# Moving twelve output products from iteration 10 of a slot into its second group, and a transfer of A's factors behind the rows of maxima

## The chip, the core and the metric

The kernel runs on one core of a Trainium2 chip. The metric is the time on the device in microseconds (us), as the median of several executions. The profile comes from one further execution, whose own time stands beside its span below. Engines are named as in the profile: PE (TensorE, matmuls), PEld (its weight loads), DVE (VectorE), ACT (ScalarE), POOL (GpSimd), and SP (SyncE), which here issues the DMAs of the main loop. A number such as L590 is a line of the kernel.

## The reference

Two attentions over the same input x (2048 rows of 512, 32 heads of 16) are mixed by a gate. A is a causal softmax attention within four chunks of 512 rows, mixed per head with a linear memory of the chunks before. B is a plain softmax attention over all 2048 rows. Each is multiplied with its output weights.

```python
def _A_ref(x, wq, wk, wv, wo, beta):
...
    for s in range(N):
        qs, ks, vs = q[:, :, s], k[:, :, s], v[:, :, s]
        logits = jnp.einsum("bhqd,bhkd->bhqk", qs, ks) * scale + mask
        p = _softmax(logits, axis=-1)
        a_dot = jnp.einsum("bhqk,bhkd->bhqd", p, vs)
        pq = phi(qs)
        num = jnp.einsum("bhld,bhde->bhle", pq, M)
        den = jnp.einsum("bhld,bhd->bhl", pq, z)[..., None] + 1e-6
        a_mem = num / den
        o = g * a_mem + (1.0 - g) * a_dot
...
    return o @ wo

def _B_ref(x, wqkv, wo):
...
    scores = jnp.einsum("bhqd,bhkd->bhqk", q, k) * (Dh ** -0.5)
    p = _softmax(scores, axis=-1)
    o = jnp.einsum("bhqk,bhkd->bhqd", p, v)
    return (lambda x, *d: x.transpose(*d))(o, 0, 2, 1, 3).reshape(B, S, D) @ wo

x = A_x
g = _sigmoid((x * gate_w).sum(-1, keepdims=True))
a = _A_ref(x, A_wq, A_wk, A_wv, A_wo, A_beta)
b = _B_ref(x, B_wqkv, B_wo)
return g * a + (1 - g) * b
```

## The kernel before

A first stage computes the projections and the memory of A and stores queries, keys and values to DRAM. Then comes the main loop (L905): 32 **slots**, k = 0 to 31. Slot k works on one unit of B (unit 32 + k) and one of A (unit k); a unit is four heads against one chunk of 512 query rows. The order of all instructions is written out by hand: the loop records them one after another, each engine executes its own in that order, and semaphores make it wait for the others. SP, too, executes its DMA issues strictly in that order.

A slot has 37 **groups** n: 32 of B (two for each of 16 blocks of 128 keys; n // 2 is the iteration "it") and five of A. For each group the loop records, in this order:

- `t_group` (L490): two score products on PE into two PSUM banks, and two exponentials on ACT (L508) that read these banks and write the probabilities. Three banks, tb, tb and mb, take turns by which was used longest ago; `misc()` hands out the same three for other work. In A's groups POOL masks the result (L511).
- what `plan` holds for the group: as a rule one `s_b` (L441), two products on PE into a double bank sbk, and a maximum over them on DVE (L450). These maxima belong to the *next* slot's unit of B; there are two double banks.
- what `extras` (L848) holds for it as "pre": in slots 9 to 31 one `out_mm` at group 2 x OMI = 20, and in slot 31 a second one at group 28.
- `pvs` (L826): the products of the probabilities with V (L524), two groups behind the scores. Group 0 has the last ones of A's unit of the slot before and then the copy of A's sums out of PSUM (L531). Group 1 has none.
- what `extras` holds as "post": `m_rows` at group 24.
- after the odd groups, `beside` (L860) and some loads.

`out_mm` (L586) is half an output projection for 128 rows: twelve products of 512 columns (L590) of oh and ol, the two halves in precision of the normalised sums, with the weights. For a = 0 (odd slots) ACT copies the result to yo (L594), for a = 1 (even slots) DVE adds the second half (L597) and SP stores yo (L598). oh and ol are made by `out_split` (L582) at the end of an even slot, by ACT and POOL.

`m_chain` (L454, recorded after group 21) turns the maxima into rows with four small DVE operations (L459 to L469), `m_rows` (L471, group 24) transposes them on PE, copies them on ACT and stores them by four DMAs (L483) into the operands of the following units.

The sums of a unit are normalised in steps: `fin_load` loads sums and denominators, `fin_rec` makes the factors and stores them to DRAM (L554), `fin_bc` (L556) loads them again, repeated over 16 partitions, into the tile d (L560), and `fin_norm` (L562) multiplies on POOL (L564; for A, from the second chunk on, it also adds B's part, L569). `beside` sets the iteration of each of these: B's `fin_bc` in iteration 6, A's in 7; `fin_norm` in even slots for B in 9 and for A in 13.

Of the kernel before, what the change touches and what calls it, by code (L numbers as in the profile page):

```python
# [26 lines left out]
EARLY = 6  # L27
S_FIRST = 10
S_LAST = 10
OMI = 10  # L30


@with_exitstack
def gated_mix_kernel(ctx, tc, x, wq, wk, wv, wo, beta, wqkv, wob, gate_w, out):
# [510 lines left out]
    def fin_rec(u):  # L545
        kd, qd, c = UN[u]
        r = AT.pop(("r", u))
        nc.vector.reciprocal(r, r)
        if kd == "A":
            nc.vector.scalar_tensor_tensor(r, r, nq[:, qd:qd + 1], grow[:, 0, c], op0=OP.mult, op1=OP.mult)  # L550
        else:
            nc.vector.tensor_tensor(r, r, grow[:, 1, c], op=OP.mult)
        AT["rd", u] = D.tile([128, E], FT, name=f"rd{u}")
        nc.sync.dma_start(AT["rd", u], r)  # L554
# [7 lines left out]
    def fin_norm(kd, g, c):  # L562
        o, d = AT["o"][c % 2][:, g, int(kd == "B")], AT["d"][int(kd == "B")]
        nc.gpsimd.tensor_tensor(o, o, d, op=OP.mult)  # L564
        if kd == "B":
            if c:
                nc.sync.dma_start(d, OM[g, c])
        elif c:
            nc.gpsimd.tensor_tensor(o, o, AT["d"][1], op=OP.add)  # L569
# [12 lines left out]
    def out_split(c, t):  # L582
        nc.scalar.activation(AT["oh"], o_cols(c, t), AF.Copy)
        nc.gpsimd.tensor_tensor(AT["ol"], o_cols(c, t), AT["oh"], op=OP.subtract)
# [19 lines left out]
    def tail_split(t, gs, a, eng=None):  # L604
        oh, ol = [x[:, gs, a] for x in tail_ops(t)]
        o = o_cols(3, t)[:, gs, a]
        if eng:
            nc.scalar.copy(oh, o)
        else:
            nc.vector.tensor_copy(oh, o)  # L610
        (eng or nc.vector).tensor_tensor(ol, o, oh, op=OP.subtract)
# [20 lines left out]
    def todo(fn, *a):  # L632
        return lambda: fn(*a)
# [86 lines left out]
    for blk in range(16):  # L720
# [12 lines left out]
        n = blk + 1 + (c == 2)  # L733
# [114 lines left out]
    def extras(k):  # L848

        pre, post = {}, {}  # L850
        if not k:
            for n in range(4):
                pre[2 * n] = [fill[n - 4]]
        post[2 * S_LAST + 4] = [todo(m_rows, k + 1)]
        for n, it in [(k - 9, OMI)] + [(23, 14)] * (k == 31):
            if n >= 0:
                pre[2 * it] = [todo(out_mm, n // 8, n // 2 % 4, n % 2)]
        return pre, post

    def beside(k, it):  # L860

        for f, it0, u in ((fin_load, NT + 1, 32 + k), (fin_rec, 5, 31 + k), (fin_bc, 6, 31 + k),
                          (fin_load, 1, k - 1), (fin_rec, 6, k - 1), (fin_bc, 7, k - 1)):
            if it == it0 and (k or it0 > NT):
                f(u)
        c, j = divmod(k - 1, 8)
        if k and j % 2:
            for kd, it0 in (("B", 9), ("A", 13)):
                if it == it0:
                    fin_norm(kd, j // 2, c)  # L870
        if k >= 8 and k % 2 == 0 and it == NT + 2:
            out_split(k // 8 - 1, k // 2 % 4)
        if (k, it) == (31, 4):
            grest = AT["grest"] = AT["o"][0][64:, 0, 0]
            nc.sync.dma_start(grest, GD[3 * C:].rearrange("(o t) -> o t", o=1).to_broadcast([64, C]))
        if (k, it) == (31, 9):
            grest = AT["grest"]
            nc.vector.tensor_scalar(grest, grest, nh[64:, 3:4], None, op0=OP.mult)
        if (k, it) == (31, NT + 2):
            fin_rec(63)  # L880
        if k == 31 and it == 13:
            o = AT["o"][1][:64, 3, 0]
            nc.gpsimd.tensor_tensor(o, o, AT["d"][0][:64], op=OP.mult)
        if k == 31 and it < 8 and it % 2 == 0:
            for a in range(2):
                tail_split(it // 2, slice(0, 3), a)


    ex = [extras(k) for k in range(32)]
    plan = {}  # L890

# [13 lines left out]
    for k in range(32):  # L905
        ua, ub = k, 32 + k
        banks = T3 + [SBK[0][:, n] for n in range(2)] * (k == 31)
        for n in range(NG):
            it = n // 2 if n < NG - 1 else NT + 2
# [6 lines left out]
            if n % 2 == 0 and n < NG - 1:  # L916
                continue
            beside(k, it)
            if it == S_LAST:
                m_chain(k + 1)  # L920
# [74 lines left out]
```

## Time and profile before

| | |
|---|---|
| time, median of 3 runs | 2007.81 us (2006.12 to 2014.9) |
| time of the profiled execution | 2007.75 us |
| its span, first to last instruction | 2006.0 us |
| granted TensorE clock | 0.995 |
| output products (L590), on banks tb and mb | 60 + 60 + 60 and 36 + 36 + 36 in the profile |
| one addition to yo on DVE (L597) | 692 ns, 12 times |
| one copy to yo on ACT (L594) | 597 ns, 12 times |
| one split on POOL (L584) | 2370 ns, 12 times |

How to read it: "busy" counts an engine's own instructions without its issues and waits. In a timeline a row is: start in us, duration in us, engine, line, operation, out<-in, shapes, count; in brackets stands the idle time of that engine just before, and what ended it. Rows of equal instructions that follow each other are merged, so a row with x2 covers the first one's start to the second one's end. Matmuls are pipelined, so the durations of PE's rows overlap.

### The profile page before, as it was taken

What the parts mean: (1) busy time and instruction counts of PE and PEld (TensorE: products, weight loads), DVE (VectorE), ACT (ScalarE), POOL (GpSimd) and SP (SyncE); (2) the same over time, 40 slices, a digit from 0 to 9 for tenths busy, and PEclk for the clock granted to TensorE, in tenths of its full rate; (3) what the DMA queues carried; (4) which work ended last, traced back from release to release, by engine and by line L of the source; (5) the groups of instructions that cost most, each with busy time, mean ns of one, the idle gap of its engine ahead of it and who ended that gap; (6) DMA issues with size and microseconds to landing.
All of it is one profiled execution on the core that took longest, in us unless ns stands there. A gap on an engine that the chain in (4) does not pass through costs nothing.

```text
span 2006.0 us, 43688 instructions
## 1 busy us (share of the span) xinstructions
PE 1956.3 (98%) x17517; PEld 949.0 (47%) x17517; DVE 1631.9 (81%) x1825; ACT 1435.1 (72%) x2703; POOL 256.6 (13%) x474
## 2 busy tenths in 40 slices
PE   8999999999999999999999999999999999999988
PEld 7777777444444344444444444444444444444434
DVE  6135665799999999999999999999899999899832
ACT  3233332688888888888787888787878787878883
POOL 2200000011110101111111111111111111111111
PEclk9999999999999999999999999999999999999999
DMA  7765656644443445343435344444444545444101
GB/s 222 164 190 177 197 180 177 148 106 112 95 112 85 104 93 109 81 110 81 109 79 112 85 112 85 112 85 112 85 112 85 112 85 111 85 112 85 50 26 54
DMA packets 162743, 222.49 MB, mean 111 GB/s; under 512 B 39261, under 2 KB 89453, under 8 KB 156781
## 3 DMA queue, kind: packets, MB, share of 16 engines
q1 hardware_dynamic: 159596, 211.70, 43.9%
q0 software_dynamic: 2944, 8.00, 2.2%
q8 instruction: 138, 2.26, 0.5%
q14 instruction: 65, 0.52, 0.1%
HBM read 148.21 MB, written 68.16 MB: 108 GB/s over the span
## 4 chain that ended last, share of the span: by engine, by line
PE 89%; DMA 3%; DVE 3%; ACT 2%; SPq 2%; issue 1%; POOL 0%; ACTq 0%; POOLq 0%; DVEq 0%
PE pvb L524 31%; PE tb L502 17%; PE sbk L448 12%; PE mb L502 8%; PE tb L279 3%; PE sbk L427 2%; PE tb L590 2%; PE mb L279 2%; ACT raw L508 2%; PE pvb L279 2%; DVE mxb L450 2%; PE sbk L430 2%; PE mb L590 1%; PE sbk L279 1%; PE tb L262 1%
## 5 line engine op out<-in xcount | busy, mean ns | idle before, releaser
L450 DVE TENSOR_REDUCE mxb<-sbk 128x2 f32<-128x1024 f32 x1024 | 1222.7, 1222 | 49.4 <-PE sbk L448 45.7
L508 ACT ACTIVATE raw<-tb 128x512 f32<-128x512 f32 x1557 | 886.0, 596 | 172.8 <-PE tb L502 85.6
L524 PE MATMUL pvb<-raw,vb 128*17 128x256 f32 (+1 forms) x8072 | 639.5, 389 | 0.0
L508 ACT ACTIVATE raw<-mb 128x512 f32<-128x512 f32 x780 | 465.2, 596 | 81.6 <-PE tb L502 57.5
L502 PE MATMUL tb<-qb,xh 64*128 64x512 f32 x880 | 330.9, 494 | 3.7 <-ACT raw L508 3.7
L524 PEld LDWEIGHTS pvb<-raw,vb 128*17 128x17 f32 x8072 | 133.8, 95 | 344.8 <-issue 338.4
L448 PE MATMUL sbk<-xh,qb 64*128 64x512 f32 x1344 | 287.6, 400 | 4.4 <-DVE mxb L450 3.3
L511 POOL TENSOR_SCALAR_AFFINE_SELECT raw<-raw 128x256 f32<-128x256 f32 (+1 forms) x320 | 115.4, 361 | 879.9 <-ACT raw L508 871.9
L502 PE MATMUL mb<-qb,xh 64*128 64x512 f32 x437 | 215.6, 493 | 2.0 <-ACT raw L508 2.0
L502 PEld LDWEIGHTS tb<-qb,xh 64*128 64x128 f32 x880 | 124.7, 183 | 190.5 <-issue 98.3
L502 PE MATMUL tb<-qb,kb 64*128 64x512 f32 x463 | 176.0, 496 | 4.8 <-ACT raw L508 2.8
L434 DVE TENSOR_REDUCE mx<-sbk 128x2 f32<-128x768 f32 (+1 forms) x128 | 139.8, 1092 | 43.9 <-PE sbk L430 36.2
L448 PE MATMUL sbk<-kb,qb 64*128 64x512 f32 x704 | 152.9, 408 | 0.8 <-DVE mxb L450 0.7
L448 PEld LDWEIGHTS sbk<-xh,qb 64*128 64x128 f32 x1344 | 138.8, 186 | 10.8 <-DVE mxb L450 7.0
L502 PEld LDWEIGHTS mb<-qb,xh 64*128 64x128 f32 x437 | 79.9, 183 | 89.5 <-issue 49.1
L502 PE MATMUL mb<-qb,kb 64*128 64x512 f32 x241 | 118.4, 491 | 0.8 <-DVE st L289 0.8
L502 PEld LDWEIGHTS tb<-qb,kb 64*128 64x128 f32 x463 | 65.8, 183 | 102.3 <-issue 51.4
L524 PE MATMUL pvb<-raw,va 128*17 128x256 f32 (+2 forms) x1280 | 94.7, 383 | 4.2 <-ACT pvs L533 0.8
L564 POOL TENSOR_TENSOR o<-o,d 128x512 f32<-128x512 f32 x31 | 39.7, 1282 | 415.2 <-DMA qa<-dA 177.0
L427 PE MATMUL sbk<-ka,qa 64*128 64x256 f32 (+3 forms) x512 | 86.6, 346 | 0.0
L502 PE MATMUL tb<-qa,ka 64*128 64x384 f32 (+3 forms) x340 | 79.5, 372 | 0.0
L448 PEld LDWEIGHTS sbk<-kb,qb 64*128 64x128 f32 x704 | 72.1, 185 | 12.6 <-issue 6.5
(265 smaller groups left out, 1804.5 us busy)
## 6 DMA issues: line engine op xcount, KB each, us to landing
xh<-dB SPq DMA_DIRECT2D x38, 512.0 KB
vb<-vdB SPq DMA_DIRECT2D x16, 1088.0 KB
dB<-st SPq DMA_DIRECT2D x64, 256.0 KB
dA<-st SPq DMA_DIRECT2D x64, 256.0 KB
pd<-pvs SPq DMA_DIRECT2D x64, 256.0 KB
kb<-dB SPq DMA_DIRECT2D x22, 512.0 KB
xh<-dB SPq DMA_DIRECT2D x38, 256.0 KB
qb<-dB SPq DMA_DIRECT2D x64, 128.0 KB
```

The costliest lines, as they stand in the source:

```text
L279: nc.tensor.matmul(b, WS[ws][w][wi][:, k, :], (XH, XL)[xi][c][:, k, :], start=n == 0, stop=n == 11)
L427: nc.tensor.matmul(b[:, j, c0:c0 + n], q_of(u)[r, p, i * 128:(i + 1) * 128], k_of(u, p)[r, :n], start=True, stop=False)
L430: nc.tensor.matmul(b[:, j, c0 + n - 128:c0 + n], crows[r, n2 - 1], cmask[r, n2 - 1], start=False, stop=n2 == 2)
L434: nc.vector.tensor_reduce(m[:, :, p, i], b[:, :, :n], axis=AX.X, op=OP.max)
L448: nc.tensor.matmul(b[:, j], q_of(u)[r, p, i * 128:(i + 1) * 128], k_of(u, p)[r, kc * C:(kc + 1) * C], start=True, stop=True)
L450: nc.vector.tensor_reduce(MXB[u][:, :, p, i, kc], b, axis=AX.X, op=OP.max)
L502: nc.tensor.matmul(bs[j][:, c0:c0 + w], k_of(u, h // 2)[r, 128 * it:128 * it + 128], q_of(u)[r, h // 2, q0:], start=True, stop=True)
L508: nc.scalar.activation(pt, bs[j], AF.Exp, scale=SCALE)
L511: nc.gpsimd.affine_select(out=m, in_=m, pattern=[[1, 128]] if n < 2 else [[0, 2], [1, 128]], compare_op=OP.is_ge, fill=0.0, base=0, channe ...
L524: nc.tensor.matmul(PVB[32 * h:32 * h + E + 1, q0 + lo:q0 + hi], vt[:, it, 4 * q + h, :], pt[:, lo:hi], start=it == 0 and lo == 0, stop=it ...
L564: nc.gpsimd.tensor_tensor(o, o, d, op=OP.mult)
L590: nc.tensor.matmul(b, (AT["oh"], AT["ol"])[oi][:, g, a], (AT["wh"], AT["wl"])[wi][:, g, a], start=n == 0, stop=n == 11)
```

## The change

```diff
-OMI = 10
+OMI = 14
...
     def extras(k):
...
-        for n, it in [(k - 9, OMI)] + [(23, 14)] * (k == 31):
+        for n, at in [(k - 9, 1)] + [(23, 2 * OMI)] * (k == 31):
             if n >= 0:
-                pre[2 * it] = [todo(out_mm, n // 8, n // 2 % 4, n % 2)]
+                pre[at] = [todo(out_mm, n // 8, n // 2 % 4, n % 2)]
...
     def beside(k, it):
...
-                          (fin_load, 1, k - 1), (fin_rec, 6, k - 1), (fin_bc, 7, k - 1)):
+                          (fin_load, 1, k - 1), (fin_rec, 6, k - 1), (fin_bc, S_LAST + 2, k - 1)):
```

The `out_mm` of slots 9 to 31 is recorded in group 1 instead of group 20. The second one of slot 31 stays at group 28. A's `fin_bc` is recorded after group 25 (iteration 12, behind `m_rows` of group 24) instead of after group 15.

PE at the start of slot 17, before: the scores of group 1 (qb, xh into mb and tb), the products for the maxima (sbk), then group 2, and only there the products with V (pvb).

```order
L524 MATMUL pvb<-raw_86,va_76 17x256 x4
L502 MATMUL mb<-qb_69,xh_88 128x512
L502 MATMUL tb_109<-qb_69,xh_88 128x512
L448 MATMUL sbk_114<-kb_89,qb_70 128x512 x2
L502 MATMUL tb_110<-qb_69,xh_88 128x512
L502 MATMUL mb<-qb_69,xh_88 128x512
L448 MATMUL sbk_113<-kb_89,qb_70 128x512 x2
L524 MATMUL pvb<-raw_86,vb_75 17x256 x4
```

The same place after the change:

```order
L524 MATMUL pvb<-raw_86,va_76 17x256 x4
L502 MATMUL mb<-qb_69,xh_88 128x512
L502 MATMUL tb_109<-qb_69,xh_88 128x512
L448 MATMUL sbk_114<-kb_89,qb_70 128x512 x2
L590 MATMUL tb_110<-wh,oh 128x512 x4
L590 MATMUL tb_110<-wl,oh 128x512 x4
L590 MATMUL tb_110<-wh,ol 128x512 x4
L502 MATMUL mb<-qb_69,xh_88 128x512
L502 MATMUL tb_109<-qb_69,xh_88 128x512
L448 MATMUL sbk_113<-kb_89,qb_70 128x512 x2
L524 MATMUL pvb<-raw_86,vb_75 17x256 x4
```

The output products now stand between the groups 1 and 2. They take the bank that the third group used first before (tb_110), and the third group (n = 2) takes the two banks of the second one (n = 1).

ACT at the same place after the change: the copy to yo stands between the exponentials of groups 1 and 2; before, it stood between those of groups 20 and 21.

```order
L508 ACTIVATE raw_86<-mb 128x512
L508 ACTIVATE raw_86<-tb_109 128x512
L594 ACTIVATE yo<-tb_110 128x512
L508 ACTIVATE raw_86<-mb 128x512
L508 ACTIVATE raw_86<-tb_109 128x512
```

DVE in an even slot before: the last maximum of a unit, the addition to yo, one more maximum, then the chain of `m_chain`. After the change the addition stands two rows behind the copy of A's sums (L531), behind the first maximum of the slot.

```order
L450 TENSOR_REDUCE mxb<-sbk_113 128x2
L597 TENSOR_TENSOR yo<-tb_110,yo 128x512
L450 TENSOR_REDUCE mxb<-sbk_114 128x2
L459 TENSOR_REDUCE mx<-mxb 128x16
L467 TENSOR_SCALAR mhi<-mx 128x32
```

SP in an even slot before: rd is the factors in DRAM, d the tiles they go to, pd the stored sums, mr the rows of maxima, qa, ka, qb and vb the operands of coming units.

```order
L560 DMA d_2836<-rd_11334 64x1x512
L554 DMA rd_11361<-rec 128x16
L369 DMA qa_74<-dA_115 32x2x512 x2
L369 DMA qa_74<-dA_115 18x2x512 x2
L369 DMA ka_72<-dA_119 16x2x512 x2
L369 DMA ka_72<-dA_119 32x2x512 x2
L560 DMA d_2835<-rd_11361 64x1x512
L567 DMA d_2836<-om_2346 128x512
L395 DMA vb_2830<-vdB 128x16x136
L598 DMA out_dram<-yo 128x512
L483 DMA qb_69<-mr 2x8x128 x2
L483 DMA qa_73<-mr 2x8x128 x2
```

After the change:

```order
L369 DMA ka_72<-dA_119 16x2x512 x2
L369 DMA ka_72<-dA_119 32x2x512 x2
L567 DMA d_2836<-om_2346 128x512
L395 DMA vb_2830<-vdB 128x16x136
L483 DMA qb_69<-mr 2x8x128 x2
L483 DMA qa_73<-mr 2x8x128 x2
L560 DMA d_2835<-rd_11375 64x1x512
```

A's factors (d_2835) now follow the four stores of the rows of maxima, and the store of yo has moved from there to the start of the slot, between the store of A's sums and their loads. POOL's instructions stand in the same order before and after.

## The prediction

> **What bounds the kernel now.** I read the page first (its busy times and its costliest groups), then who waited for whom, then one slot of the main loop on each engine in order of time.
>
> ```profile
> span 2006.0 us, 43688 instructions
> PE 1956.3 (98%) x17517; PEld 949.0 (47%) x17517; DVE 1631.9 (81%) x1825; ACT 1435.1 (72%) x2703; POOL 256.6 (13%) x474
> L450 DVE TENSOR_REDUCE mxb<-sbk 128x2 f32<-128x1024 f32 x1024 | 1222.7, 1222 | 49.4 <-PE sbk L448 45.7
> ...
> PE tb L502 <- ACT raw L508: 6.2, 22, 0.3
> ```
>
> PE is busy 98% of the span. The last line is from the list of waits, for PE between 450 and 1950 us (total, times, longest): PE almost never stands idle there, but 22 times it waits up to 0.3 us for ScalarE's exponentials. Where these waits stand decides this case, so I measure a slot. VectorE's copy of A's sums (L531) runs once a slot, near its start; the copies of slots 5, 6, 17 and 18 on VectorE's timeline (start, duration) give the slots' lengths:
>
> ```profile
> 610.18 0.68 DVE L531 COPY pvs<-pvb 128x512 f32<-128x512 f32 x1
> ...
> 658.18 0.68 DVE L531 COPY pvs<-pvb 128x512 f32<-128x512 f32 x1
> ...
> 1211.60 0.68 DVE L531 COPY pvs<-pvb 128x512 f32<-128x512 f32 x1
> ...
> 1262.58 0.68 DVE L531 COPY pvs<-pvb 128x512 f32<-128x512 f32 x1
> ```
>
> A slot without output products takes 658.18 - 610.18 = 48.00 us, one with them 1262.58 - 1211.60 = 50.98. So **the products cost 2.98 us a slot where they stand**. PE's timeline there, in slot 17:
>
> ```profile
> 1234.97 0.61 PE L448 MATMUL sbk<-xh,qb 64*128 64x512 f32 x2
> 1235.51 1.21 PE L590 MATMUL tb<-wh,oh 128*128 128x512 f32 x4
> 1236.56 1.09 PE L590 MATMUL tb<-wl,oh 128*128 128x512 f32 x4
> 1237.48 1.08 PE L590 MATMUL tb<-wh,ol 128*128 128x512 f32 x4
> 1238.49 0.63 PE L524 MATMUL pvb<-raw,vb 128*17 128x256 f32 x8
> ```
>
> The twelve products occupy PE from 1235.51 to 1238.49, 2.98 us: the same number. Nothing of them is hidden in iteration 10, because PE's work is packed there without a gap.
>
> **The change, part one: the products in the second group.** The same twelve products, the same copy or addition and the same store are issued, only earlier: no work is added or removed. What differs is what PE does at the new place. Slot 17's first groups, PE's timeline:
>
> ```profile
> 1211.64 0.40 PE L448 MATMUL sbk<-kb,qb 64*128 64x512 f32 x2
> 1211.87 0.39 PE L502 MATMUL tb<-qb,xh 64*128 64x512 f32 x1
> 1212.54 0.49 PE L502 MATMUL mb<-qb,xh 64*128 64x512 f32 x1 [0.28 <-ACT raw L508]
> 1212.55 0.71 PE L448 MATMUL sbk<-kb,qb 64*128 64x512 f32 x2
> ...
> 1211.89 0.60 ACT L508 ACTIVATE raw<-mb 128x512 f32<-128x512 f32 x1 [0.39 <-PE tb L502]
> 1212.39 1.08 ACT L508 ACTIVATE raw<-tb 128x512 f32<-128x512 f32 x2
> ```
>
> The second group ends with the scores of 1211.64, and has no products with V behind it. The third group's second score product (1212.54) needs bank mb, which ScalarE reads from 1211.89 to 1212.49. So PE has a hole, and the output products go exactly there. In iteration 10 the first product starts 0.54 us after its pair of scores; that pair is drawn out to 0.61 against 0.40 here, so I take 0.40: first product 1212.04, block 2.98, third group at 1215.02, both halves at once, since their banks are long free. Now its last half starts at 1212.54: a delay of 2.48 us in place of 2.98. **Saved: 0.50 us a slot.** The bounds are 0 (the hole closes otherwise) and 0.67 (both halves of the third group would go at 1211.87 if no bank were missing: 1212.54 - 1211.87).
>
> In odd slots ScalarE copies the product out of its bank, an operation of the size of an exponential (0.60). That copy now precedes the third group's exponentials. Last product done about 1215.1, copy to 1215.7, exponentials starting 0.5 apart (1211.89, 1212.39): the first ends at about 1216.2, when the fourth group wants its bank (1215.02 + 1.22, since a group takes as long as its reduction). That costs 0 to 0.2; I take 0.1. In even slots VectorE's addition comes instead; the slot's first reduction, behind the copy at 1211.60, is over by about 1213.5 (0.68 + 1.22), and the next one waits for scores, so I cost it at nothing; its cover is gone if VectorE is still reducing when the products end, at most the 0.69 us of the addition. Slots 9 to 30: 11 x 0.50 + 11 x 0.40 = **9.9 us**. In slot 31 there are no reductions, so its rows differ; one block moves within it, for which I take 0, between -2.98 and +2.98.
>
> The products read oh and ol, split at the end of the slot before. Does the wait move there? POOL's timeline has
>
> ```profile
> 1210.35 2.37 POOL L584 TENSOR_TENSOR ol<-o,oh 128x1024 fp32r<-128x1024 f32 x1 [0.55 <-ACT oh L583]
> ```
>
> so ol is ready at 1212.72, and only the last four products read it, from 1212.04 + 1.97 = 1214.01 (1237.48 - 1235.51 above): 1.3 us to spare. The store of yo moves on SP ahead of the loads of A's sums; in slot 18 these wait for the landing of A's own store until 1273.61, long after an addition that would end at about 1267:
>
> ```profile
> 1263.29 0.34 SPq L535 DMA_DIRECT2D pd<-pvs  x1
> 1273.61 0.52 SPq L541 DMA_DIRECT2D o<-pd  x1
> ```
>
> **Part two: A's factors behind the rows of maxima.** Slot 26 is long. Its copies of A's sums, then VectorE, POOL and PE inside it:
>
> ```profile
> 1670.51 0.68 DVE L531 COPY pvs<-pvb 128x512 f32<-128x512 f32 x1
> ...
> 1723.04 0.68 DVE L531 COPY pvs<-pvb 128x512 f32<-128x512 f32 x1
> ...
> 1700.04 0.76 DVE L467 TENSOR_SCALAR mhi<-mx 128x32 fp32r<-128x32 f32 x1
> 1700.92 1.28 DVE L469 SCALAR_TENSOR_TENSOR m<-mx,mhi 128x32 f32<-128x32 f32 x1
> ...
> 1693.23 1.28 POOL L564 TENSOR_TENSOR o<-o,d 128x512 f32<-128x512 f32 x1 [24.53 <-DMA ka<-dA]
> 1699.48 1.28 POOL L564 TENSOR_TENSOR o<-o,d 128x512 f32<-128x512 f32 x1 [4.97 <-DMA d<-rd]
> 1700.84 1.32 POOL L569 TENSOR_TENSOR o<-o,d 128x512 f32<-128x512 f32 x1
> ...
> 1703.39 0.50 PE L448 MATMUL sbk<-xh,qb 64*128 64x512 f32 x2 [1.34 <-DVE mxb L450]
> ```
>
> The slot takes 52.53 us, 1.55 over 50.98. The chain of maxima (L467 to L469) is stretched until POOL's scaling of A's sums is done (0.76 ends at 1700.80 against POOL's 1700.76; 1.28 ends at 1702.20 against 1702.16), the reductions slip behind it, and PE waits 1.34 us. Over all slots from 450 to 1925 us (groups: busy, mean ns; and above them minimum, median, maximum):
>
> ```profile
> L467 DVE TENSOR_SCALAR mhi<-mx x31: 181/182/1165, 444.8 to 1935.7; 128x32 fp32r<-128x32 f32 x31
> L469 DVE SCALAR_TENSOR_TENSOR m<-mx,mhi x31: 179/185/1278, 445.1 to 1936.0; 128x32 f32<-128x32 f32 x31
> ...
> L467 DVE TENSOR_SCALAR mhi<-mx 128x32 fp32r<-128x32 f32 x29 | 9.6, 331 | 1.0
> L469 DVE SCALAR_TENSOR_TENSOR m<-mx,mhi 128x32 f32<-128x32 f32 x29 | 6.4, 222 | 0.0
> ```
>
> Against the medians that is 29 x (0.331 - 0.182) + 29 x (0.222 - 0.185) = 4.3 + 1.1 = 5.4 us of stretching. Not all of it reaches PE (in slot 26, 0.58 + 1.10 = 1.68 became 1.55), and the first slots keep POOL's work on the output weights. The change puts A's transfer behind the chain, so its scaling can't meet the chain any more. B's scaling could: in slot 26 it ends at 1694.51, and moves 2.5 later with the groups that prepare it, while the chain at 1700.04 moves 0.5 earlier; 2.5 us remain between them. I take **4 us**, between 0 and 5.4.
>
> [...]
>
> Where A's scaling goes, from slot 16 (SP, POOL, and a window with DMA share and GB/s last):
>
> ```profile
> 1182.08 0.53 SPq L560 DMA_DIRECT2D d<-rd  x1
> ...
> 1194.76 1.03 SPq L483 DMA_DIRECT2D qa<-mr  x2
> ...
> 1187.23 1.27 POOL L564 TENSOR_TENSOR o<-o,d 128x512 f32<-128x512 f32 x1 [5.04 <-DMA d<-rd]
> 1188.58 1.28 POOL L569 TENSOR_TENSOR o<-o,d 128x512 f32<-128x512 f32 x1
> 1203.20 0.29 POOL L511 TENSOR_SCALAR_AFFINE_SELECT raw<-raw 128x128 f32<-128x128 f32 x1 [13.34 <-ACT raw L508]
> ...
> 1194.00:1196.00 2.00, 2.00 (x23) 0.71 (x24) 1.93 (x3) 1.61 (x4) 0.00 (x0) 1.00 0.04 10
> ```
>
> Now 5.15 us pass from A's issue to POOL's start. Put behind the rows' stores it is issued at 1195.8; at 5.15 the scaling runs from 1200.9 to 1203.6, against the masks' first at 1203.20. On nearly idle queues (share 0.04) it should be shorter, and the masks are used a group or two later. Behind POOL's waiting scaling stand only masks and the split. I cost it at nothing.
>
> **The sum.** 9.9 + 4 = 13.9 us off this execution's 2007.75 us (span 2006.0), which is at the median 2007.81: **1994 us**.
>
> **The rivals.** First, PE is simply full: 98% busy means that the products cost 2.98 us anywhere, and only the chain's 4 us go: 2004. The hole at 1212.54 speaks against it. [...] Second, A's part brings nothing, because B's scaling or another POOL task takes its place at the chain: the products' 9.9 alone, 1998. Third, the other side: POOL runs late at the slot's end. If A's factors land over 9 us after their issue, scaling, masks, split and ol slip together, and PE, which now wants ol 1.3 us after it is ready, waits in every odd slot and at the masks in every even one. Landing takes 5.15 us with a large load beside it, so this needs 4 us more; a slip of 2 us beyond the slack in 15 slots is 30 us: 2024. [...]
>
> **Chances.** Forecast 0.66 (its own range 1990 to 1998), PE full 0.14, no gain from A's part 0.11, slower 0.09. The range reaches from all bounds on the good side (22 x 0.67 + 5.4 = 20.1) to PE full: 1988 to 2004. A change of 0.5% (10 us) is about what a measurement here can tell from none: faster, under 1998, is the forecast and half of the case without A's part, 0.71; within 0.5% 0.20; slower 0.09.
>
> **What would show it.** Right: the distance of the copies L531 at about 50.4 us, no PE wait before the third group's second half, products at group two some 2.98 us long, L467 and L469 at their medians in even slots, POOL's scaling of A ending before the masks. Wrong: products waiting for ol, PE waiting for masks, or a slot of 50.9 with the products at the new place.

## The result, and the profile after

| | before | after |
|---|---|---|
| median, us (6 runs each) | 2008.95 | 1993.69 |
| range, us | 2006.12 to 2015.15 | 1992.13 to 1996.79 |
| profiled execution: time, us | 2007.75 | 1993.86 |
| its span, us | 2006.0 | 1992.1 |

The ratio is 0.9921, 95% interval 0.9907 to 0.9936: faster by 0.8%, by 15.3 us between the medians and by 13.9 between the profiled executions. Forecast were 13.9 and 1994.

The busy times of the whole profile, after:

```profile
PE 1948.7 (98%) x17517; PEld 944.6 (47%) x17517; DVE 1631.2 (82%) x1825; ACT 1436.5 (72%) x2703; POOL 257.5 (13%) x474
```

The shares are those of before: 98% for PE in both. From this line nobody would see that anything was to be had. It is seen in the slots. VectorE's timeline after (start, duration), with the copies of A's sums of slots 17, 18 and 19:

```profile
1208.76 0.68 DVE L531 COPY pvs<-pvb 128x512 f32<-128x512 f32 x1
...
1259.15 0.68 DVE L531 COPY pvs<-pvb 128x512 f32<-128x512 f32 x1
...
1309.59 0.68 DVE L531 COPY pvs<-pvb 128x512 f32<-128x512 f32 x1
```

The odd slot 17 takes 50.39 against 50.98, the even slot 18 takes 50.44. Slot 5, without products, still takes 48.02. So the products now cost some 2.4 us a slot instead of 2.98, and odd and even slots are alike.

The place itself: slot 17 after, PE's, ScalarE's and POOL's timelines (start, duration, line, operation; in brackets an idle time ahead of it and what ended it):

```profile
1208.80 0.40 PE L448 MATMUL sbk<-kb,qb 64*128 64x512 f32 x2
1209.12 1.19 PE L590 MATMUL tb<-wh,oh 128*128 128x512 f32 x4
...
1211.07 1.07 PE L590 MATMUL tb<-wh,ol 128*128 128x512 f32 x4
1212.07 0.50 PE L502 MATMUL mb<-qb,xh 64*128 64x512 f32 x1
1212.07 0.49 PE L502 MATMUL tb<-qb,xh 64*128 64x512 f32 x1
...
1213.28 0.50 PE L502 MATMUL tb<-qb,xh 64*128 64x512 f32 x1
...
1212.17 0.60 ACT L594 ACTIVATE yo<-tb 128x512 f32<-128x512 f32 x1 [2.03 <-PE tb L590]
1212.67 0.59 ACT L508 ACTIVATE raw<-mb 128x512 f32<-128x512 f32 x1
...
1207.50 2.38 POOL L584 TENSOR_TENSOR ol<-o,oh 128x1024 fp32r<-128x1024 f32 x1 [0.55 <-ACT oh L583]
```

The products run from 1209.12 to 1212.07, 2.95 us. Behind them both halves of the third group start together at 1212.07; before, the second half waited 0.28 us for a bank. ol is done at 1209.88 and first read at 1211.07. ScalarE's copy goes ahead of the exponential, which ends at 1213.26; the fourth group starts at 1213.28, one step of 1.21 us behind the third, so nothing is late there.

Between 450 and 1925 us, the list of waits (total, times, longest) and the groups of the chain of maxima (busy, mean ns):

```profile
PE tb L502 <- ACT raw L508: 2.0, 7, 0.3
```

```profile
L467 DVE TENSOR_SCALAR mhi<-mx 128x32 fp32r<-128x32 f32 x30 | 6.0, 199 | 1.0
...
L469 DVE SCALAR_TENSOR_TENSOR m<-mx,mhi 128x32 f32<-128x32 f32 x30 | 5.5, 184 | 0.0
```

Before, this list had 22 such waits of 6.2 us on the banks tb and, in a row of its own, 7 of 2.0 us on mb: one in each of the slots 2 to 30. What is left are 7, all before 804 us, in slots without output products; in the slots 9 to 30 the wait is gone from every one. The means of the chain fell from 331 and 222 ns to 199 and 184; only in the slots 1 (ahead of this stretch) and 3 is it still stretched.

Summed over the trace, slot by slot (first exponential to first exponential), the 13.9 us are (slot 0 and what precedes it cancel; slot 31 is taken to its last exponential):

| place | us gained |
|---|---|
| slots 9 to 30: an undisturbed slot 50.92 before, 50.39 after, 22 x 0.53 | 11.7 |
| slots 9 to 30: the rest of their 15.3, mostly stretched chains that are gone (slot 26 alone: 52.54 to 50.40) | 3.6 |
| slots 1 to 8: -1.2 in slot 1, -0.6 in slot 3, -1.5 in slot 8, +0.7 in slot 6 | -2.7 |
| slot 31: 50.59 to 49.21 | 1.4 |

Of the 3.6 us, 3.3 lie in the slots whose chain was stretched before (10, 12, 24, 26 and 28). Slots 13 and 14 give some 0.5 that is not the chain's: they took 51.26 and 51.18 with their chains at the medians. Slot 20 gives 0.3 less than the others.

### The profile page after: what moved, and what is told of

It reads as the page before. It is cut to its first block, busy times and chain, and to the rows that moved or that the text cites. A ratio compares the mean times of both kernels' runs of the same rounds, so it can differ in the third digit from the quotient of the medians.

```text
span 1992.1 us, 43657 instructions
## 1 busy us (share of the span) xinstructions
PE 1948.7 (98%) x17517; PEld 944.6 (47%) x17517; DVE 1631.2 (82%) x1825; ACT 1436.5 (72%) x2703; POOL 257.5 (13%) x474
## 4 chain that ended last, share of the span: by engine, by line
PE 87%; DMA 5%; DVE 2%; issue 2%; ACT 2%; SPq 1%; POOL 0%; ACTq 0%; POOLq 0%; DVEq 0%
PE pvb L524 31%; PE tb L502 17%; PE sbk L448 12%; PE mb L502 8%; PE tb L279 3%; PE sbk L427 2%; PE tb L590 2%; PE mb L279 2%; PE sbk L430 2%; DVE mxb L450 1%; PE mb L590 1%; PE pvb L279 1%; ACT raw L508 1%; DMA pd<-pvs 1%; DMA vdA<-vb 1%
## 5 line engine op out<-in xcount | busy, mean ns | idle before, releaser
L450 DVE TENSOR_REDUCE mxb<-sbk 128x2 f32<-128x1024 f32 x1024 | 1226.2, 1222 | 38.3 <-PE sbk L448 33.9
L448 PE MATMUL sbk<-xh,qb 64*128 64x512 f32 x1344 | 283.0, 398 | 2.4 <-DMA xh<-dB 1.1
L502 PE MATMUL mb<-qb,xh 64*128 64x512 f32 x445 | 219.6, 494 | 0.0
L564 POOL TENSOR_TENSOR o<-o,d 128x512 f32<-128x512 f32 x31 | 39.8, 1283 | 563.3 <-DMA d<-rd 301.8
```

Source lines behind the costliest of these rows:

```text
L448: nc.tensor.matmul(b[:, j], q_of(u)[r, p, i * 128:(i + 1) * 128], k_of(u, p)[r, kc * C:(kc + 1) * C], start=True, stop=True)
L450: nc.vector.tensor_reduce(MXB[u][:, :, p, i, kc], b, axis=AX.X, op=OP.max)
L502: nc.tensor.matmul(bs[j][:, c0:c0 + w], k_of(u, h // 2)[r, 128 * it:128 * it + 128], q_of(u)[r, h // 2, q0:], start=True, stop=True)
```

## The experiments

All edits are to the changed kernel. The theory: the products cost less only between groups 1 and 2, since PE has a hole only there; the chain of maxima is stretched whenever POOL's scaling meets it. Rivals: PE's work got shorter for some other reason; the chain's part is worth nothing; the transfer, not the scaling, disturbs the chain.

**The products alone** (A's factors go back to the place before):

```diff
-(fin_load, 1, k - 1), (fin_rec, 6, k - 1), (fin_bc, S_LAST + 2, k - 1)):
+(fin_load, 1, k - 1), (fin_rec, 6, k - 1), (fin_bc, 7, k - 1)):
```

> The products in group 1, A's factors still in iteration 7. Theory (the two parts lean on each other): a slot with products costs 48.0 + 2.4 us as in the changed kernel, but A's scaling on POOL now starts about 2.4 us later in the slot and the chain of maxima 0.5 us earlier, so they meet in most even slots instead of in five: mean of L467 over 450 to 1925 us above 331 ns, time 1998 to 2003. Rival (the parts simply add): the chain is hit as often as before, L467 about 331 ns, time about 1997, which is the changed kernel's 1993.7 plus the 4 us of the chain less what its slots 1 and 3 lose.

Measured: 2004.89 us (10 runs), ratio 0.9977, interval 0.9962 to 0.9993. This is a miss: just outside what I had expected, and only 4.1 us better than the 2009.02 of the kernel before beside it. Its groups of the chain and its waits between 450 and 1925 us:

```profile
L469 DVE SCALAR_TENSOR_TENSOR m<-mx,mhi 128x32 f32<-128x32 f32 x29 | 14.1, 486 | 0.0
L467 DVE TENSOR_SCALAR mhi<-mx 128x32 fp32r<-128x32 f32 x29 | 10.9, 376 | 1.0
```

```profile
PE sbk L448 <- DVE mxb L450: 11.9, 10, 1.8
```

The odd slots take 50.4 us, so the hole is gained in full. But the chain is stretched in all even slots from 12 to 26, more than before the change (means 376 and 486 ns against 331 and 222), and PE waits for it. These eight slots take 51.2 to 53.7 us, together 14.3 more than eight of 50.4. Slot 14 shows why; first the kernel before, then the products alone (SP's issue of A's factors, POOL's scaling, VectorE's chain):

```profile
1079.82 0.53 SPq L560 DMA_DIRECT2D d<-rd  x1
...
1084.97 1.29 POOL L564 TENSOR_TENSOR o<-o,d 128x512 f32<-128x512 f32 x1 [4.69 <-DMA d<-rd]
1086.33 1.29 POOL L569 TENSOR_TENSOR o<-o,d 128x512 f32<-128x512 f32 x1
...
1088.40 0.18 DVE L467 TENSOR_SCALAR mhi<-mx 128x32 fp32r<-128x32 f32 x1
```

```profile
1080.21 0.53 SPq L560 DMA_DIRECT2D d<-rd  x1
...
1085.91 1.27 POOL L564 TENSOR_TENSOR o<-o,d 128x512 f32<-128x512 f32 x1 [5.49 <-DMA d<-rd]
1087.26 1.31 POOL L569 TENSOR_TENSOR o<-o,d 128x512 f32<-128x512 f32 x1
...
1085.97 1.25 DVE L467 TENSOR_SCALAR mhi<-mx 128x32 fp32r<-128x32 f32 x1
...
1087.35 1.27 DVE L469 SCALAR_TENSOR_TENSOR m<-mx,mhi 128x32 f32<-128x32 f32 x1
...
1089.81 0.49 PE L448 MATMUL sbk<-xh,qb 64*128 64x512 f32 x2 [1.81 <-DVE mxb L450]
```

Before, the chain started 8.58 us behind the issue of the factors (1088.40 - 1079.82), when the scaling was done (1087.62). In iteration 10 the products stood between the two. With them gone the chain starts 5.76 us behind it (1085.97 - 1080.21), 2.82 sooner, and falls into the scaling: L467 ends at 1087.22 and L469 at 1088.62, within 0.05 us of the ends of POOL's L564 (1087.18) and L569 (1088.57). The products had been keeping the two apart, and the change's second part is needed for the first.

**The factors alone** (the products back in iteration 10):

```diff
-for n, at in [(k - 9, 1)] + [(23, 2 * OMI)] * (k == 31):
+for n, at in [(k - 9, 20)] + [(23, 2 * OMI)] * (k == 31):
```

> A's factors behind the rows of maxima, the products still in group 20. Theory (POOL's scaling stretched the chain): L467 and L469 are at their medians of 0.18 us in all even slots from 6 on, slots with products take 50.9 us each without exception, slots 1 and 3 are longer by some 1.2 and 0.6 us as in the changed kernel, time about 2005. Rival (the products ahead of the chain are what stretches it): L467 stays near a mean of 331 ns and the time near 2008.

Measured: 2006.31 us (10 runs), ratio 0.9991 (0.9976 to 1.0007): not told from no change. Groups of the chain, 450 to 1925 us, and the copies of slots 17 and 18:

```profile
L469 DVE SCALAR_TENSOR_TENSOR m<-mx,mhi 128x32 f32<-128x32 f32 x29 | 6.4, 222 | 0.0
L467 DVE TENSOR_SCALAR mhi<-mx 128x32 fp32r<-128x32 f32 x29 | 5.3, 182 | 1.0
```

```profile
1212.77 0.68 DVE L531 COPY pvs<-pvb 128x512 f32<-128x512 f32 x1
...
1263.73 0.68 DVE L531 COPY pvs<-pvb 128x512 f32<-128x512 f32 x1
```

The chain is clean from slot 4 on (one L469 of 1.28 us is left, in slot 3), and the slot takes 50.96: the products cost what they did. Two details missed what I had expected. Slots 13, 14 and 26 take 51.2 with clean chains, and why stays open; and of the first slots only slot 3 is longer, by 0.8 us, while slot 1 takes 48.01. One part alone gives 4.1 us, the other 2.7 (which may be nothing), both together 15.3. The parts do not add: the upper ends of the two intervals, 7.6 and 4.8 us, sum to 12.4, and the lower end for both together is 12.9. The slots' sums say why: the first part alone gains 11.7 from the hole, while its stretched chains cost 14.3 in place of some 3.6. That leaves 1.0 us in this profile; the ten runs scatter from 1998.40 to 2007.65.

**One group later, and one earlier** (one execution each, so read by the slots and not by the time):

```diff
-for n, at in [(k - 9, 1)] + [(23, 2 * OMI)] * (k == 31):
+for n, at in [(k - 9, 2)] + [(23, 2 * OMI)] * (k == 31):
```

> The products one group later than in the changed kernel, in group 2, behind the wait for the exponentials. Theory (the hole ahead of group 2's scores hides 0.5 us of them): the hole is back, products cost 2.9 to 3.0 us, slots 9 to 29 take 50.9 us, time about 2005. Rival (what cost time was iteration 10 itself, just ahead of the chain): slots stay at 50.4 us, time about 1994.

Measured: 2007.10 us. Copies of slots 17 and 18, and the wait for the exponentials between 450 and 1925 us:

```profile
1211.56 0.68 DVE L531 COPY pvs<-pvb 128x512 f32<-128x512 f32 x1
...
1262.59 0.68 DVE L531 COPY pvs<-pvb 128x512 f32<-128x512 f32 x1
```

```profile
PE tb L502 <- ACT raw L508: 6.2, 22, 0.3
```

A slot of 51.03 (50.95 in the median of the slots 9 to 30), and the 22 waits are back: one group later the products cost their 2.98 us again, and PE's time is not shorter by itself. With 0 in place of the 1:

> The products one group earlier, in group 0. Theory (the hole): the products stand ahead of the hole and do not fill it, slots take 50.9 us, time about 2005; the products' last four start about 2.4 us into the slot where ol is ready at 2.3, so at most 0.1 us of waiting for POOL in odd slots. Rival (any place at the start of the slot does): 50.4 us, about 1994. Rival (ol): odd slots longer than even ones by 0.5 us and more.

Measured: 2010.52 us. Waits between 450 and 1925 us:

```profile
PEld tb L590 <- POOL ol L584: 2.4, 7, 0.3
...
PEld mb L590 <- POOL ol L584: 1.4, 4, 0.4
...
PE tb L502 <- ACT raw L508: 6.3, 22, 0.3
```

Here the hole stays open, behind the products: odd slots take 51.1 to 51.3 us, even ones 50.9 to 51.2. In the 11 odd slots PE's weight load waits for ol, 0.35 us on average (3.8 / 11), where I had allowed 0.1 at most; the odd slots are some 0.2 us longer than the even ones, less than the rival's 0.5. So ol's margin in the changed kernel is real: one group earlier it is gone. The position between groups 1 and 2 is the only one of the four tried at which the products cost less than their 2.98 us.

**The scaling late, the transfer early.** To tell the scaling from its transfer, the factors go back (as in the products alone) and A's `scale` is recorded late:

```diff
-(fin_load, 1, k - 1), (fin_rec, 6, k - 1), (fin_bc, S_LAST + 2, k - 1)):
+(fin_load, 1, k - 1), (fin_rec, 6, k - 1), (fin_bc, 7, k - 1)):
...
-for kd, it0 in (("B", 9), ("A", 13)):
+for kd, it0 in (("B", 9), ("A", 16)):
```

> Products in group 1, A's factors loaded in iteration 7 as before the change, but A's scaling on POOL recorded in iteration 16, behind the masks of two groups. Only POOL's order differs from the run with the products alone; SP's queue is the same. Theory (POOL's scaling beside the chain is the cause, not the transfer): the chain is at its medians, slots with products 50.4 us, time 1994 to 1997; a little more than the changed kernel if the later masks come late. Rival (the transfer ahead of the rows of maxima is the cause): the time stays near 2005 and L467 near its mean of 376 ns.

Measured: 1999.74 us (4 runs), ratio 0.9951 (0.9932 to 0.9970). Groups of the chain and waits between 450 and 1925 us, and POOL's timeline at the end of slot 18:

```profile
L469 DVE SCALAR_TENSOR_TENSOR m<-mx,mhi 128x32 f32<-128x32 f32 x29 | 5.4, 185 | 0.0
L467 DVE TENSOR_SCALAR mhi<-mx 128x32 fp32r<-128x32 f32 x29 | 5.3, 182 | 1.0
```

```profile
PEld pvb L524 <- POOL raw L511: 15.8, 64, 0.3
```

```profile
1304.02 1.27 POOL L569 TENSOR_TENSOR o<-o,d 128x512 f32<-128x512 f32 x1
1305.24 2.20 POOL L511 TENSOR_SCALAR_AFFINE_SELECT raw<-raw 128x256 f32<-128x256 f32 x6
1307.51 2.37 POOL L584 TENSOR_TENSOR ol<-o,oh 128x1024 fp32r<-128x1024 f32 x1
```

The transfer stands where it stood with the products alone, and the chain is at its medians: the scaling stretches it, not the transfer. The time misses what I had expected (1994 to 1997), though; it is 6.8 us above the changed kernel beside it (1992.98, below). The run thereby prices a late POOL: scaling, masks and split follow each other without a gap, and the even slots 10 to 28 take 51.0 to 51.1 us instead of 50.4, 0.7 each, which for these ten is about the whole difference. In the changed kernel weight loads wait for masks 30 times (7.5 us), here 64 times (15.8). That is what the change itself avoids, in slot 26 barely: there the scaling ends at 1705.09, and the first mask follows without a gap (its record starts at 1705.05).

**The weights' loads early.** Slots 1 and 3 became longer with the change. After, slot 1, VectorE, POOL, PE:

```profile
445.54 1.28 DVE L469 SCALAR_TENSOR_TENSOR m<-mx,mhi 128x32 f32<-128x32 f32 x1
...
445.46 1.30 POOL L577 TENSOR_TENSOR wl<-o,wh 128x512 fp32r<-128x512 f32 x1
...
448.01 0.50 PE L448 MATMUL sbk<-kb,qb 64*128 64x512 f32 x2 [1.14 <-DVE mxb L450]
```

POOL's casts of the output weights now meet the chain: L469 ends at 446.82, wl at 446.76. These loads follow `fin_bc` on SP before the change and precede it after, so the casts start earlier. Moving the loads to iteration 2 should free the chain:

```diff
+            if it == 2 and 1 <= k <= 4:
+                load_wo(k - 1)
             if it == NT and k < 29:
...
-                if 1 <= k <= 4:
-                    load_wo(k - 1)
```

> The changed kernel with the loads of the output weights (slots 1 to 4) recorded in iteration 2 instead of 9, so that POOL's casts of them come before the chain of maxima. Theory (slots 1 and 3 of the changed kernel are long because these casts, which now start earlier, meet the chain): slots 1 to 4 take 48.0 us each, L467, L468 and L469 stay at 0.18 us in them, about 1.8 us less than the changed kernel in the profile, which the time cannot tell. Rival (those slots wait for the weights' DMAs or for jitter): slots 1 and 3 stay at 49.2 and 48.6.

Measured: 1992.51 us (4 runs), ratio 0.9915 (0.9894 to 0.9936). Copies of slots 1 and 2, and L467 over the whole run (minimum, median, maximum in ns):

```profile
418.96 0.68 DVE L531 COPY pvs<-pvb 128x512 f32<-128x512 f32 x1
...
467.15 0.68 DVE L531 COPY pvs<-pvb 128x512 f32<-128x512 f32 x1
```

```profile
L467 DVE TENSOR_SCALAR mhi<-mx x33: 181/181/183, 321.8 to 1922.1; 128x32 fp32r<-128x32 f32 x33
```

Slot 1 takes 48.19 (slots 2 and 3 take 47.99 and 48.01), and no chain is stretched anywhere. Slot 4 missed what I had expected: it takes 48.75. There POOL's work on the weights now meets another short operation, VectorE's scaling of the factors (L550, 0.23 us elsewhere):

```profile
579.97 1.07 DVE L550 SCALAR_TENSOR_TENSOR rec<-rec,nq,grow 128x16 f32<-128x16 f32 x1
...
579.73 1.28 POOL L577 TENSOR_TENSOR wl<-o,wh 128x512 fp32r<-128x512 f32 x1
```

The two end at 581.04 and 581.01. So the move frees the chain, but in one slot of four it only changes what is hit. The run's profiled span, 1990.7, is the shortest of all. Against the changed kernel beside it the medians differ by 0.5 us, which these runs do not tell apart.

**The changed kernel once more**, beside the last two:

> The changed kernel once more, beside the two others on the same chip: about 1994; by the theory of the hole its slots with products take 50.4 us in this execution too, and slot 31 is 49.2 us where PE's clock stays whole in it and about 50.5 where it is halved for one window.

Measured: 1992.98 us (4 runs), ratio 0.9918 (0.9898 to 0.9937). Slots 9 to 30 sum to 1107.6 us, against 1107.7 in the first profile; slot 31 takes 50.43 instead of 49.21 (below). Slots 1 and 3 are long again, 48.87 and 48.76.

## Why the prediction was right, step by step

- **The hole behind the second group's scores: right, a little larger.** 0.53 us a slot against 0.50. The prediction's line of 22 waits covered the banks tb alone; with bank mb there were 29, one a slot from slot 2 on. Both halves of the third group start together behind the products, as forecast, and only this position gives it (the runs one group on, one back, and in iteration 10).
- **ScalarE's copy in odd slots: 0.1 forecast, nothing found.** Counted from the score products ahead of them (1208.80), the output products began and ended some 0.1 us sooner than I had placed them, so the exponential ends 0.02 us before the fourth group starts. The hole's term is therefore 22 x 0.53 = 11.7 where the sum had 9.9.
- **The addition in even slots and ol: nothing, as forecast.** Slot 18 takes 50.44; ol is done 1.19 us before it is read, where 1.3 was forecast.
- **The chain: 4 forecast.** 3.3 in slots 9 to 30 and 0.7 in slot 6, beside some 0.3 in slots 9 to 30 that no chain explains. The scaling, not the transfer, was the cause, by the run that kept the transfer and moved the scaling. B's scaling stays clear of the chain, as forecast: it ends 4.7 to 6.1 us ahead of it in the even slots 10 to 28, where 2.5 was reckoned, and 1.2 us ahead in slot 30.
- **That the two parts add: wrong, though the sum held.** I priced the chain at what it cost before the change. The products alone raise that price to 14.3 us, since they had held the chain off the scaling. The second rival (A's part brings nothing: 1998) was priced by the same step. Undoing A's part gave 2004.89, not 1998: its part beside the products is worth some 11 us.
- **The first slots: not in the sum.** The prediction let the first slots "keep POOL's work on the output weights", but moving `fin_bc` brought the weights' loads forward, and slots 1 and 3 lost 1.8 us. The run with earlier loads shows it. To that extent the second rival came true: another POOL task took the scaling's place at the chain. Slot 8 lost 1.5 more, behind VectorE's wait of 1.6 us for a late load of the denominators (tile rec); this slot took between 48.0 and 49.6 in the kernels of this study, longer where that wait was longer (48.1 in the kernel before, with no such wait; 49.6 after). Why the load comes late is open.
- **Slot 31: 0 forecast, 1.4 found.** Most of it is the clock (below): with the products still in group 20 but a whole clock, in the run of the factors alone, the slot took 49.39. So the move itself gave about 0.2, and 1.2 is not the change's.
- **The rivals.** PE full: excluded, the products cost 2.4 us and not 2.98. POOL late: did not happen (in the even slots 10 to 28 the scaling starts 3.6 to 4.7 us behind its issue, where 5.15 was assumed); where it was made to happen it cost 0.7 us per even slot, far from the 2 us in 15 slots that the rival assumed. For the reductions that now run beside A's scaling the sum had nothing, and they paid nothing: the 53 that overlap a scaling after 800 us average 1222 ns, the others there 1223.

That the forecast and the profiled execution agree to 0.1 us is luck: misses of +1.8 (hole), +0.3 (the unexplained part of slots 9 to 30), -3.4 (first slots and slot 8) and +1.4 (slot 31) nearly cancel.

## What to carry to other kernels

A busy share of 98% does not say that no place is cheaper (here one place was cheaper by 0.53 us a slot): look for the group whose second half starts late because of a bank, and put independent work of the same engine ahead of it. Before moving a block, ask also what its old place kept apart. A block between a transfer's issue and another engine's short, critical operations can be a spacer (with the products moved alone, the stretched chains cost 14.3 us in place of some 3.6), and the two parts of such a change have to be priced together. Where VectorE's short operations sit on PE's path, keep POOL's long ones off them (L467, 0.18 us alone, took 1.25 beside a scaling of 1.27), by order and not by the luck of a landing, and look at all of them: moved off one, a long operation can land on the next (L550, 0.23 us alone, took 1.07 beside a cast of 1.28).

## What the hardware showed that I had not expected

**TensorE's clock was halved for 3.4 us behind some short stalls.** A stall is here a stretch in which PE stands idle. With the products alone, slots 12 and 14 took 53.4 and 53.7 us, though PE stalled there for only 1.39 and 1.81 us. Slot 14 in stretches of 2 us (length; busy time of PE, its weight loads, VectorE, ScalarE and POOL, with counts; granted clock; DMA share; GB/s):

```profile
1089.50:1091.50 2.00, 1.69 (x18) 0.85 (x18) 2.00 (x3) 0.27 (x1) 0.00 (x0) 1.00 0.00 0
1091.50:1093.50 2.00, 2.00 (x15) 0.66 (x12) 1.65 (x2) 1.08 (x2) 0.00 (x0) 0.51 0.03 8
1093.50:1095.50 2.00, 2.00 (x14) 0.49 (x12) 1.23 (x1) 1.11 (x3) 0.00 (x0) 0.63 0.03 8
```

The 0.51 and 0.63 are a granted clock at half from about 1091.5 to 1095.0, some 1.7 us behind the stall's end at 1089.81, and whole for the rest. That is about 1.5 us on top of the stall (slot 14: 3.3 over 50.4, less 1.81), and one reason why the products alone did worse than I expected. In slot 12 the two stretches of 2 us from 985.5, where the stall ends, have a granted clock of 0.56 and 0.59, again 3.4 us at half, and the next one has 1.00. It doesn't follow every such stall: in the kernel before, a stall of 1.46 us ends at 1941.22, in the changed kernel two of 1.46 us end at 1920.07 and 1931.73, and in the stretches of 2 us behind all three the clock is at 1.00.

Slot 31 has it too. In the kernel before, a stall of 1.95 us ends there at 1928.31, and the clock is 0.50 from 1930 to 1932 (0.84 and 0.81 in the stretches of 2 us before and after, so 3.4 us at half). With the factors alone the same stall, 1.95 us to 1927.25, left the clock at 1.00 (over the whole execution it is 0.997, as in the changed kernel; the kernel before has 0.995), and the slot took 49.39 us instead of 50.59. PE's timeline at the same place in the changed kernel, and in the changed kernel once more:

```profile
1920.07 0.49 PE L502 MATMUL sbk<-qb,xh 64*128 64x512 f32 x1 [1.46 <-ACT raw L508]
```

```profile
1919.27 0.50 PE L502 MATMUL sbk<-qb,xh 64*128 64x512 f32 x1 [1.46 <-ACT raw L508]
```

And the stretch behind each stall, in the same order:

```profile
1920.00:1922.00 2.00, 1.94 (x14) 0.62 (x14) 1.87 (x7) 1.10 (x3) 0.00 (x0) 1.00 0.05 4
```

```profile
1920.00:1922.00 2.00, 2.00 (x12) 0.50 (x4) 1.90 (x6) 0.89 (x2) 0.00 (x0) 0.52 0.05 4
```

The same program with the same stall of 1.46 us keeps a whole clock in one execution (slot 31: 49.21 us) and drops to half in another (50.43). So the clock was halved behind stalls of 1.39 to 1.95 us, some of the time; what decides it, no run here shows.
